# Attention denominators divided in the tail by rows spread through DRAM, and sigmoid gates computed in the prologue

## The chip, the cores and the metric

The kernel runs on one core of one Trainium2 chip. The metric is the device time of one execution in microseconds. The core has a matrix engine (TensorE; PE in the profile, PEld its weight loads), three engines for elementwise work (VectorE = DVE, ScalarE = ACT, GpSimd = POOL) and a queue engine that here only issues transfers (SyncE = SP; SPq for its DMA queue). Each engine works through its own instructions in order and waits on semaphores.

## What is computed

For a prompt of S = 2048 rows and D = 512 columns, with H = 32 heads of 16, a sliding window of 256, and a feed-forward part of F = 1792:

```python
q, k, v = split_heads(x @ wqkv)
scores = einsum("bhqd,bhkd->bhqk", q, k) * (Dh ** -0.5)
p = softmax(where((0 <= i - j) & (i - j < 256), scores, -1e9))
a = merge_heads(p @ v) @ wo                        # attention
b = (silu(x @ w_gate) * (x @ w_up)) @ w_down       # feed-forward
g = sigmoid((x * gate_w).sum(-1, keepdims=True))   # one gate per row
out = g * a + (1 - g) * b
```

## The kernel before

Everything is in float32, with operands split into a high and a low part, so that a product takes three matmuls (`mm3`, `products`). There are 16 blocks of 128 rows (NB), 4 column chunks of 512 (NCH, CH) and 8 groups of 4 heads (G). The order of each engine is the order in which the Python code issues its instructions; nothing reorders them later.

**Prologue (about 0 to 85 us).** x is loaded transposed, chunk by chunk, into the buffers that later hold the second pair of query and key stacks (slots `q10`, `q11`, `k10`, `k11`), and `split_x(c)` makes high and low parts of chunk c on ScalarE and VectorE. `proj` computes queries and keys for the first two head groups. `stack(g, hf)` writes their rows into the stacked layout by twelve transfers on SyncE. Then `stage1(0, ·)` starts: per block and head one scores matmul into a PSUM bank, then one VectorE instruction (line 304, `CUSTOM_DVE`) that masks it in place and takes the row maximum. For group 0 the four heads of a block alternate between two pools of two banks, so four score results can stand at a time; the matmul of the next block needs the bank of the block before. The value projections of the later blocks are interleaved.

**Main loop (to about 600 us).** It runs over t = 0 .. 128, 16 steps to a group. In a step `stage1` of the next group and `stage2` of this one (scores again with the maximum folded in, exponential on ScalarE, window cut on GpSimd) alternate with pieces of the feed-forward matmuls (line 252). Every fourth step `av` multiplies the probabilities with the values. The value tile has a column of ones, so row DH = 16 of each head's 32 rows is the softmax denominator. `finish(g, c)` takes the result of one chunk out of PSUM (lines 380 and 382), transposes it (386), divides by the denominator (390, 391), transposes it back (394) and writes it to DRAM, `od` (395, on GpSimd's queue). The function `later(t, hd, f)` puts work at a step t and a head position hd. In the last groups it places 16 gate blocks (line 631: a row block of x times gate_w, summed) and then `gate_end`, which makes the sigmoid and its complement and writes both to DRAM, `gd`.

**Tail (from about 600 us).** TensorE begins with the four `last_tile` products of the feed-forward part, 24 matmuls each. Meanwhile SyncE loads `wo`, the attention results (`load(e)`, from `od`) and the gate row spread over all partitions (`gates(0)`, 1 MB). `halve(e)` splits a loaded attention piece into high and low (ScalarE cast `hh`, VectorE subtraction `hl`), four items ahead of its use. The 16 items of `multiply_a` follow, twelve matmuls each, which TensorE starts at 622.77; `attn` multiplies their results by the gate (line 905) on VectorE and sends them to the output. Then come the items of the down projection, whose results `scaled` multiplies by 1 - gate (line 945) and adds into the output by the transfer.

```python
def load(e):
    _, c, k = e
    heads = od[2 * k:2 * k + 2].rearrange("g (j e) s -> (g j) e s", e=32)
    SRC[e] = taken(heads[:, :DH, c * CH:(c + 1) * CH])
```

An item's source is thus eight heads of sixteen rows, 512 columns each.

Of the kernel before, what the change touches and what calls it, by code (L numbers as in the profile page):

```python
# [16 lines left out]
P = 128  # L17
# [3 lines left out]
CH = 512  # L21
# [15 lines left out]
def gated_mix(ctx, tc, xT, xn, wqk, wv, wo, wgu, wd, gw, outT):  # L37
# [117 lines left out]
    gd = dram.tile([32, 4, 32], F32, name="gd")  # L155

# [44 lines left out]
    with ExitStack() as A:  # L201
# [170 lines left out]
        def finish(g, c):  # L372
# [5 lines left out]
            both, ot = AB[::-1] if c % 2 else AB  # L378
# [4 lines left out]
            if lo:  # L383
                nc.vector.tensor_copy(both[:, :lo], first[:, :lo])
            yield
            nc.vector.transpose(ot, both)
            yield
            v = ot.rearrange("p (s e) -> p s e", e=32)
            rc = osb.tile([P, CH // 32], F32, name="rc")
            nc.vector.reciprocal(rc, v[:, :, DH])  # L390
            nc.vector.tensor_tensor(out=v[:, :, :DH], in0=v[:, :, :DH],
                                    in1=rc[:, :, None].to_broadcast([P, CH // 32, DH]), op=ALU.mult)
            yield
            nc.vector.transpose(both, ot)
# [95 lines left out]
        split_x(2)  # L490
        for b in range(2, 4):
            run(vproj(b))
        run(proj(0, 1, pp, "pa"))
        stack(0, 0)
        split_x(3)
        QT.append([slot(f"q1{pr}") for pr in range(2)])
        KT.append([slot(f"k1{pr}") for pr in range(2)])
        for hf in range(2):
            fill_rows(QT[1], 0.0, hf, nc.gpsimd)
            fill_rows(KT[1], 1.0, hf, nc.gpsimd)  # L500
        run(proj(1, 1, pp, "pa"))
        for c in range(2, NCH):
            run(proj(0, c, pp, "pa"))
        stack(0, 1)
        stack(1, 0)

# [113 lines left out]
        XG = []  # L620

        def gate_place():
            xh, xl = x_pair()
            XG.extend(h.bitcast(F32) for t in (xh, xl) for h in halves_of(t))
            nc.sync.dma_start(XG[0], gw[None, :].to_broadcast([P, D]))

        def gate_fetch(b):
            nc.sync.dma_start(XG[2 + b % 2], xn[b * P:(b + 1) * P])

        def gate_block(b):  # L630
            nc.vector.scalar_tensor_tensor(XG[1], XG[2 + b % 2], 1.0, XG[0], op0=ALU.mult, op1=ALU.mult,
                                           accum_out=gate[:, b:b + 1])

# [24 lines left out]
        def gate_end():  # L658
            nc.scalar.activation(gate, gate, AF.Exp, scale=-1.0)
            nc.vector.tensor_scalar(gate, gate, 1.0, None, op0=ALU.add)  # L660
            nc.vector.reciprocal(gate, gate)
            nc.vector.tensor_scalar(igate, gate, -1.0, 1.0, op0=ALU.mult, op1=ALU.add)
            rows, cols = (sm.tile([P, 32], F32, name=n, bufs=1) for n in ("mt", "mtt"))
            nc.vector.tensor_copy(rows[:, :NB], gate)
            nc.vector.tensor_copy(rows[:, NB:], igate)
            nc.vector.transpose(cols, rows)
            nc.sync.dma_start(gd.rearrange("c q i -> q c i"), cols)

        blocks = [(t, n) for t in range(g7 - 8, g7 + NB, 4) for n in (range(1, 3) if t < g7 else range(3))][:NB]
        blocks = [(t + n, 3 - (n > 0)) for t, n in blocks]  # L670
        later(g7 - 11, 1, gate_place)
        for b in range(NB):
            t, hd = blocks[b]
            later(t, hd, lambda b=b: gate_block(b))
            if b > 1:
                t, hd = blocks[b - 2]
                later(t + hd // 3, (hd + 1) % 4, lambda b=b: gate_fetch(b))
            else:
                later(g7 - 10 + b, 2, lambda b=b: gate_fetch(b))
        later(g7 + NB - 2, 3, gate_end)  # L680
        for k in range(4):
            early(k)

        later(g7 + NB - 1, 3, lambda: later(g7 + NB, 0, prepare))
# [416 lines left out]
```

## Time and profile before

| what | value |
|---|---|
| median of 3 runs | 806.98 us (806.5 to 807.97) |
| the profiled execution | 805.57 us, its span 803.9 us |
| TensorE busy | 798.0 us (99%) |
| VectorE busy | 626.9 us (78%) |
| ScalarE busy | 432.4 us (54%) |
| GpSimd busy | 346.0 us (43%) |
| granted TensorE clock | 1.00 |
| DMA | 121.88 MB, mean 152 GB/s |

Rows of instruction groups read: line, engine, operation, output<-input, shape, count | busy us, mean ns of one | idle time of the engine ahead of them. Rows of the timeline read: start, duration, engine, line, operation, count [idle time ahead <- what ended it]. Rows of waits read: engine and its output <- engine that it waited for: total us, times, longest.

### The profile page before, as it was taken

The numbers are of one execution on the slowest core, as the hardware profiler recorded it, in microseconds if no ns is written. First come the engines' busy times: TensorE is split into PE (matmuls) and PEld (weight loads), VectorE is DVE, ScalarE is ACT, GpSimd is POOL, SyncE is SP. The second block draws the span as 40 slices with busy tenths as digits, with TensorE's granted clock in tenths as the row PEclk, the third lists the DMA queues.
The fourth block names the chain that finished last, engine by engine and source line by source line (L and its number), as shares of the span: only waits on it lengthen the run. The fifth ranks groups of instructions, "written<-read, shape, count | busy, mean of one in ns | idle before, by whom it ended". The sixth has DMA issues, their size and how long they took to land.

```text
span 803.9 us, 21546 instructions
## 1 busy us (share of the span) xinstructions
PE 798.0 (99%) x8251; PEld 679.7 (85%) x8251; DVE 626.9 (78%) x1685; ACT 432.4 (54%) x882; POOL 346.0 (43%) x647
## 2 busy tenths in 40 slices
PE   9999999999999999999999999999999999999997
PEld 7888998889888888888888988888878888888886
DVE  6397787868887787878777878888675478899896
ACT  7422556665566567555666556545643235554642
POOL 8812546555545456544656454546740111000212
PEclk9999999999999999999999999999999999999999
DMA  8584514435252453351444516435627898728535
GB/s 301 167 226 137 140 68 133 121 102 147 68 155 77 117 167 97 116 156 52 133 118 131 151 43 202 131 102 172 203 93 236 265 345 304 293 71 271 95 54 104
DMA packets 61963, 121.88 MB, mean 152 GB/s; under 512 B 10852, under 2 KB 19556, under 8 KB 61604
## 3 DMA queue, kind: packets, MB, share of 16 engines
q1 hardware_dynamic: 54756, 99.27, 40.2%
q0 software_dynamic: 7104, 21.24, 9.1%
q8 instruction: 65, 1.06, 0.6%
q14 instruction: 38, 0.31, 0.1%
HBM read 55.97 MB, written 39.34 MB: 119 GB/s over the span
## 4 chain that ended last, share of the span: by engine, by line
PE 98%; DVE 2%; issue 0%; POOL 0%; POOLq 0%
PE pa L252 24%; PE pb L252 24%; PE pb L365 7%; PE ps L302 6%; PE ps L341 5%; PE ps L88 4%; PE ps L89 4%; PE ps L90 4%; PE pa L232 2%; PE pb L232 2%; PE ps L365 2%; PE pb L88 2%; PE pa L88 2%; PE pa L89 2%; PE pb L89 2%; PE pb L90 2%
## 5 line engine op out<-in xcount | busy, mean ns | idle before, releaser
L304 DVE CUSTOM_DVE_ANT_0 ps<-ps,mask 128x384 f32<-128x384 f32 (+2 forms) x512 | 268.4, 540 | 102.4 <-PE ps L341 51.4
L343 ACT ACTIVATE pt<-ps 128x384 f32<-128x384 f32 (+2 forms) x512 | 238.0, 474 | 130.1 <-PE ps L302 66.3
L345 POOL TENSOR_SCALAR_AFFINE_SELECT pt<-pt 128x256 f32<-128x256 f32 x256 | 109.4, 428 | 200.2 <-ACT pt L343 199.7
L341 PE MATMUL ps<-q,k 64*128 64x384 f32 (+2 forms) x512 | 161.3, 333 | 0.0
L302 PE MATMUL ps<-k,q 63*128 63x384 f32 (+2 forms) x512 | 159.3, 331 | 0.5 <-DVE mx L304 0.5
L252 PE MATMUL pb<-xhi,wh 64*128 64x512 f32 x512 | 114.7, 395 | 0.0
L252 PE MATMUL pb<-xlo,wh 64*128 64x512 f32 x512 | 113.3, 391 | 0.0
L252 PE MATMUL pb<-xhi,wl 64*128 64x512 f32 x512 | 113.3, 391 | 0.0
L252 PE MATMUL pa<-xhi,wh 64*128 64x512 f32 x512 | 113.2, 394 | 0.0
L252 PE MATMUL pa<-xlo,wh 64*128 64x512 f32 x512 | 111.8, 391 | 0.0
L252 PE MATMUL pa<-xhi,wl 64*128 64x512 f32 x512 | 111.8, 391 | 0.0
L302 PEld LDWEIGHTS ps<-k,q 63*128 63x128 f32 x512 | 88.7, 184 | 17.1 <-issue 5.7
L348 POOL TENSOR_SCALAR_AFFINE_SELECT pt<-pt 128x256 f32<-128x256 f32 x224 | 98.4, 439 | 0.0
L341 PEld LDWEIGHTS ps<-q,k 64*128 64x128 f32 x512 | 90.5, 184 | 5.8 <-issue 0.8
L365 PE MATMUL ps<-pt,vg 64*32 64x320 f32 (+4 forms) x1408 | 75.0, 346 | 0.0
L365 PE MATMUL pb<-pt,vg 64*32 64x320 f32 (+3 forms) x1360 | 73.9, 350 | 0.0
L304 DVE DVE_READ_ACCUMULATOR2_ANT mx<- 128x1 f32 x512 | 71.4, 139 | 0.0
L365 PEld LDWEIGHTS pb<-pt,vg 64*32 64x32 f32 x1360 | 46.4, 106 | 28.1 <-DVE mx L304 5.1
L252 PEld LDWEIGHTS pb<-xhi,wh 64*128 64x128 f32 x512 | 60.4, 185 | 5.4 <-DVE o L382 0.2
L252 PEld LDWEIGHTS pb<-xhi,wl 64*128 64x128 f32 x512 | 60.1, 184 | 4.9
L252 PEld LDWEIGHTS pa<-xhi,wl 64*128 64x128 f32 x512 | 58.7, 184 | 5.5
L252 PEld LDWEIGHTS pa<-xhi,wh 64*128 64x128 f32 x512 | 58.7, 186 | 3.7
(305 smaller groups left out, 1629.8 us busy)
## 6 DMA issues: line engine op xcount, KB each, us to landing
kept_h<-ev SPq DMA_DIRECT2D x52, 256.0 KB
od<-o POOLq DMA_DIRECT2D x32, 256.0 KB, 3.8
raw<-wgu SPq DMA_DIRECT2D x28, 256.0 KB
q<-xhi SPq DMA_DIRECT2D x56, 128.0 KB
k<-xhi SPq DMA_DIRECT2D x56, 128.0 KB
outT<-sg POOLq DMA_DIRECT2D x28, 256.0 KB, 4.0
vd<-vs POOLq DMA_DIRECT2D x8, 672.0 KB, 4.8
vg<-vd SPq DMA_DIRECT2D x32, 168.0 KB
```

The lines of the kernel that those rows point to most:

```text
L88: nc.tensor.matmul(ps, lh, rh, start=start and i == 0, stop=False, skip_group_check=skip)
L89: nc.tensor.matmul(ps, lh, rl, start=False, stop=False, skip_group_check=skip)
L90: nc.tensor.matmul(ps, ll, rh, start=False, stop=stop and i == n - 1, skip_group_check=skip)
L232: nc.tensor.matmul(ps, w, x, start=n == 0, stop=n == len(todo) - 1)
L252: mm = nc.tensor.matmul(ps[me], w[r], x[r], start=not second and i == 0, stop=bool(second) and i == n - 1)
L302: nc.tensor.matmul(ps[:, :n], QT[g % 2][pr][r, q0:q0 + P], KT[g % 2][pr][r, k0:k0 + n], start=True, stop=True)
L304: mx = nc.vector.tensor_tensor_reduce(out=ps[:, :n], in0=ps[:, :n], in1=mask[:, 3 * P - n:], scale=1.0, scalar=NEG, op0=ALU.add, op1=ALU.m ...
L341: nc.tensor.matmul(ps[:, :n], KT[g % 2][pr][r, k0:k0 + P], QT[g % 2][pr][r, k0:k0 + n], start=True, stop=True)
L343: BEHIND.append(nc.scalar.activation(pt[:, j, :n], ps[:, :n], AF.Exp, scale=SCALE))
L345: nc.gpsimd.affine_select(out=pt[:, :, :P], in_=pt[:, :, :P], pattern=[[0, 2], [1, P]], compare_op=ALU.is_ge, fill=0.0, base=0, channel_mu ...
L348: nc.gpsimd.affine_select(out=pt[:, :, 2 * P:], in_=pt[:, :, 2 * P:], pattern=[[0, 2], [-1, P]], compare_op=ALU.is_ge, fill=0.0, base=-1, ...
L365: nc.tensor.matmul(AV[g, c][h][32 * j:32 * j + 32, q0 - c * CH:q1 - c * CH], VG[4 * g + kb // 4][o, kb % 4, 17 * j:17 * j + 32], PT[g, kb, ...
```

## The change

`finish` no longer transposes and divides: it writes the undivided sums with the denominators to `od`. For each group three new steps run one after another: `get_den` reads the denominators of four heads from `od` into a tile of 128 x 64, `invert_den` takes the reciprocal and multiplies it by the gate (`grow`, laid out alike), `put_den` writes the result to DRAM, `rd`, one row per head. For groups 0 to 6 this happens in the main loop after the group; for group 7 in the tail. In the tail, `inverse(e)` loads eight rows of `rd`, each spread over 16 partitions, and `halve(e)` multiplies the attention piece by it before splitting. `attn` becomes a ScalarE copy, and `gates(0)` with its 1 MB load goes.

Since the gate is now needed early, it is computed in the prologue. The slot `q10` serves as gate_w and three fetch buffers (`gx`), so its fill with zeros moves behind `gate_end`. Nine gate blocks stand behind `split_x(2)`, seven behind `split_x(3)`.

```diff
+    rd = dram.tile([H, S], F32, name="rd")
+    def get_den(g):
+        nc.sync.dma_start(den, od[g].rearrange("(j e) (u s) -> j e u s", e=32, s=64)[:, DH])
+    def invert_den():
+        nc.vector.reciprocal(den, den)
+        nc.vector.tensor_tensor(out=den, in0=den, in1=grow, op=ALU.mult)
+    def put_den(g):
+        nc.sync.dma_start(rd[4 * g:4 * g + 4].rearrange("j (u s) -> j u s", s=64), den)
...
-            nc.vector.transpose(ot, both)
-            v = ot.rearrange("p (s e) -> p s e", e=32)
-            rc = osb.tile([P, CH // 32], F32, name="rc")
-            nc.vector.reciprocal(rc, v[:, :, DH])
-            nc.vector.tensor_tensor(out=v[:, :, :DH], in0=v[:, :, :DH],
-                                    in1=rc[:, :, None].to_broadcast([P, CH // 32, DH]), op=ALU.mult)
-            nc.vector.transpose(both, ot)
             nc.gpsimd.dma_start(od[g, :, c * CH:(c + 1) * CH], both)
...
         split_x(2)
+        gx = [h for t in halves_of(slot("q10", F32)) for h in halves_of(t)]
+        nc.sync.dma_start(gx[0], gw[None, :].to_broadcast([P, D]))
+        def gate_blocks(bs, ahead):
+            for b in bs:
+                t = gx[1 + b % 3]
+                nc.vector.scalar_tensor_tensor(t, t, 1.0, gx[0], op0=ALU.mult, op1=ALU.mult, accum_out=gate[:, b:b + 1])
+                if b + 3 < ahead:
+                    gate_fetch(b + 3)
+        for b in range(3):
+            gate_fetch(b)
+        gate_blocks(range(9), 9)
         for b in range(2, 4):
             run(vproj(b))
         run(proj(0, 1, pp, "pa"))
         stack(0, 0)
+        for b in range(9, 12):
+            gate_fetch(b)
         split_x(3)
+        gate_blocks(range(9, NB), NB)
...
+        gate_end()
         stack(0, 1)
         stack(1, 0)
+        nc.sync.dma_start(grow, gd[:NB].rearrange(...))
...
+        for g in range(G - 1):
+            t = (g + 1) * NB
+            later(t + 4, 2, lambda g=g: get_den(g))
+            later(t + 6, 2, invert_den)
+            later(t + 7, 2, lambda g=g: put_den(g))
...
+        def inverse(e):
+            _, c, k = e
+            z_place(4 * (c % 2), 0)
+            SRC[e] = SRC[e], PLACE["z", 2 * (c % 2)][:, k]
+            nc.sync.dma_start(SRC[e][1],
+                              rd[8 * k:8 * k + 8, c * CH:(c + 1) * CH][:, None].to_broadcast([8, DH, CH]))
...
         for e in ITEMS[:LEAD]:
             load(e)
-        gates(0)
+        for e in ITEMS[:LEAD - 1]:
+            inverse(e)
         store = last_tile(0)
...
+        get_den(G - 1)
         last_tile(1)
+        invert_den()
         store()
+        put_den(G - 1)
         for f in late[2:]:
             f()
+        for e in ITEMS[LEAD - 1:AHEAD]:
+            inverse(e)
...
+            if n + 8 < WO:
+                inverse(ITEMS[n + 8])
```

How the order of the engines moves: in the rows below, the numbers of buffers stand behind the names; `k_...` on the right are the raw x chunks, `ps_...` the PSUM banks of the scores. VectorE in the prologue, from the third x split to the first score maximum, before:

```order
L73 TENSOR_TENSOR xlo_76<-k_145,xhi_75 128x512 x4
L73 TENSOR_TENSOR xlo_78<-k_146,xhi_77 128x512 x4
L304 ISA ps_474,mx<-ps_474,mask 128x128
L304 ISA mx 128x1
L304 ISA ps_477,mx<-ps_477,mask 128x128
```

The same stretch of VectorE now (line 316 is the former 304):

```order
L73 TENSOR_TENSOR xlo_76<-k_148,xhi_75 128x512 x4
L504 SCALAR_TENSOR_TENSOR q_297,gate<-q_297 128x512 x9
L73 TENSOR_TENSOR xlo_78<-k_149,xhi_77 128x512 x4
L504 SCALAR_TENSOR_TENSOR q_297,gate<-q_297 128x512 x7
L510 TENSOR_SCALAR gate<-gate 128x16
L511 RECIPROCAL gate<-gate 128x16
L512 TENSOR_SCALAR igate<-gate 128x16
L514 COPY mt<-gate 128x16
L515 COPY mt<-igate 128x16
L516 STREAM_TRANSPOSE mtt<-mt 128x32
L316 ISA ps_522,mx<-ps_522,mask 128x128
```

The sixteen gate blocks and the six operations of `gate_end` now stand ahead of the first score maximum.

SyncE in the tail, from its first load on, before:

```order
L738 DMA got<-wo 128x512 x4
L738 DMA got<-od 128x1x512 x4
L890 DMA k_10639<-gd 128x2048
L738 DMA got<-od 128x1x512 x2
L776 DMA kept_h<-q_10667 128x512
L738 DMA got<-od 128x1x512 x4
L776 DMA kept_h<-q_10667 128x512
L738 DMA got<-od 128x1x512 x2
L185 DMA xlo_10821<-wd 128x512 x2
```

SyncE in the tail now (`rd` the spread inverse rows, `den` the denominators of the last group):

```order
L744 DMA got<-wo 128x512 x4
L744 DMA got<-od 128x1x512 x4
L839 DMA q_10510<-rd 128x1x512 x3
L744 DMA got<-od 128x1x512 x2
L160 DMA den<-od 128x1x64
L782 DMA kept_h<-q_10540 128x512
L167 DMA rd<-den 128x64
L839 DMA q_10510<-rd 128x1x512
L839 DMA k_10592<-rd 128x1x512 x2
L744 DMA got<-od 128x1x512 x4
L782 DMA kept_h<-q_10540 128x512
L839 DMA k_10592<-rd 128x1x512 x2
```

The load of `den` is the fourteenth transfer of the tail, and the spread loads stand between the loads of `od`.

VectorE in the tail, from the second `last_tile` on, now:

```order
L780 SCALAR_TENSOR_TENSOR k_10579<-k_10579,pa 128x512
L781 SCALAR_TENSOR_TENSOR k_10579<-k_10579,pb 128x512
L163 RECIPROCAL den<-den 128x64
L164 TENSOR_TENSOR den<-den,grow 128x64
L73 TENSOR_TENSOR wol<-got,woh 128x512 x2
L780 SCALAR_TENSOR_TENSOR q_10540<-q_10540,pa 128x512
L781 SCALAR_TENSOR_TENSOR q_10540<-q_10540,pb 128x512
L846 TENSOR_TENSOR got<-got,q_10510 128x512
L73 TENSOR_TENSOR hl<-got,hh 128x512
L846 TENSOR_TENSOR got<-got,q_10510 128x512
```

Before, the lines 163, 164 and 846 were not there; the two `wol` splits followed the second `last_tile` at once.

More of the change, by code (lines that the diff above doesn't have):

```diff
@@ L155, in gated_mix @@
     gd = dram.tile([32, 4, 32], F32, name="gd")
+    rd = dram.tile([H, S], F32, name="rd")
+    grow, den = (const.tile([P, 64], F32, name=n) for n in ("grow", "den"))
+    def get_den(g):
[5 more added lines that the diff above has]
+        nc.sync.dma_start(rd[4 * g:4 * g + 4].rearrange("j (u s) -> j u s", s=64), den)
     def half_sign(f, c):
@@ L503, in gated_mix @@
             run(proj(0, c, pp, "pa"))
+        gate_end()
+        for hf in range(2):
+            fill_rows(QT[1][:1], 0.0, hf, nc.gpsimd)
         stack(0, 1)
         stack(1, 0)
+        nc.sync.dma_start(grow, gd[:NB].rearrange("c q i -> (c q i)").rearrange("(u s) -> u s", s=64)[None].to_broadcast([4, 32, 64]))
         first = chain(*(stage1(0, b) for b in range(NB)))
@@ L619, in gated_mix @@
         g7 = (G - 1) * NB
[L620 to L632, printed above, removed]
         def early(k):
@@ L656, in early @@
             later(t - 1, 2, lambda: later(t, 3, rest))
[L658 to L680, printed above, removed]
+        for g in range(G - 1):
[3 more added lines that the diff above has]
+            later(t + 7, 2, lambda g=g: put_den(g))
         for k in range(4):
@@ L999, in gated_mix @@
             halve(e)
+        for e in ITEMS[AHEAD:8]:
+            inverse(e)
         rows = [(p, k) for p in ORDER if p in STAGES for k in range(4, NP)]
```

44 lines of the change are left out of this document (29 added, 15 removed).

## The prediction

> **What bounds the kernel now.** I read the busy times and the granted clock first, then the chain that ended last, then the waits.
>
> ```profile
> PE 798.0 (99%) x8251; PEld 679.7 (85%) x8251; DVE 626.9 (78%) x1685; ACT 432.4 (54%) x882; POOL 346.0 (43%) x647
> PEclk9999999999999999999999999999999999999999
> PE 98%; DVE 2%; issue 0%; POOL 0%; POOLq 0%
> PE ps L302 <- DVE mx L304: 0.5, 2, 0.2
> ```
>
> TensorE is busy for 798.0 of 803.9 us at full clock, and the chain lies on it for 98%. The change touches none of its instructions, so it can only shorten or lengthen TensorE's waits. The last row (time, count, longest) says how little there is to shorten: in all the main loop TensorE stood visibly still for VectorE twice, 0.5 us together. VectorE, at 78%, is not the bound. A place where TensorE must wait for a new chain is therefore a loss at almost full price, and there are two candidates: the prologue and the start of the tail.
>
> **Part 1, taken out of `finish` (main loop).** These are the groups that go, busy time and mean ns:
>
> ```profile
> L386 DVE STREAM_TRANSPOSE o<-o 128x512 f32<-128x512 f32 x32 | 22.6, 705 | 0.0
> L394 DVE STREAM_TRANSPOSE o<-o 128x512 f32<-128x512 f32 x32 | 22.5, 703 | 0.2
> L391 DVE TENSOR_TENSOR o<-o,rc 128x256 f32<-128x256 f32 x32 | 17.0, 531 | 1.1
> L390 DVE RECIPROCAL rc<-o 128x16 f32<-128x16 f32 x32 | 7.9, 248 | 0.0
> ```
>
> That is 22.6 + 22.5 + 17.0 + 7.9 = 70.0 us of VectorE, 2.19 us for each of 32 pieces. What TensorE gets of it is only the stalls that these instructions cause. The timeline has the largest kind:
>
> ```profile
> 201.11 1.15 DVE L391 TENSOR_TENSOR o<-o,rc 128x256 f32<-128x256 f32 x1
> 202.23 0.39 PE L252 MATMUL pa<-xhi,wl 64*128 64x512 f32 x2
> 202.85 0.44 PE L302 MATMUL ps<-k,q 63*128 63x384 f32 x1 [0.23 <-DVE mx L304]
> ```
>
> One multiplication took 1.15 instead of 0.53 us, the maximum behind it came late, and the next scores matmul began at 202.85 instead of 202.23 + 0.23 (its neighbours follow at 0.23): 0.39 us lost. Twice that is 0.8. A start-to-start gap that is a little long isn't listed as a wait; I allow 0.4 for those. Bounds: 0 (other VectorE work takes the blame) to 3. I take **-1.2**. Seven small reciprocals, seven multiplications (each at most the 0.25 of L390) and their 14 small transfers come back, in a loop that has just lost 2.19 us of VectorE at 28 places: nothing. The transposed-out piece reaches `od` 2 us sooner, which nobody waits for until the tail. The 16 gate blocks leave the last groups, where TensorE did not wait for them: nothing.
>
> **Part 2, gates in the prologue.** VectorE now does, between the third and fourth x split, nine gate blocks, then behind the fourth split seven more, then `gate_end`'s exponential on ScalarE and six operations of VectorE, and only then the first maximum (L304 of before). SyncE issues fetches 9 to 11 only behind the twelve `stack` transfers.
>
> ```profile
> 9.91 4.80 SPq L465 DMA_DIRECT2D k<-xT  x8
> 15.14 0.33 SPq L78 DMA_DIRECT2D raw<-wgu  x1
> 34.29 0.59 SPq L286 DMA_DIRECT2D k<-xhi  x1
> 1.25 0.42 SPq L465 DMA_DIRECT2D q<-xT  x1
> 3.96 0.62 ACT L70 CAST xhi<-q 128x512 fp32r<-128x512 f32 x1 [0.86 <-DMA q<-xT]
> L631 DVE SCALAR_TENSOR_TENSOR xhi<-xlo,xhi 128x512 f32<-128x512 f32 x16 | 11.0, 690 | 1.7 <-DMA xlo<-xn 1.7
> L631 DVE DVE_READ_ACCUMULATOR xhi<-xlo,xhi 128x1 f32 x16 | 1.3, 79 | 0.0
> 594.33 0.07 DVE L631 DVE_READ_ACCUMULATOR xhi<-xlo,xhi 128x1 f32 x1
> 596.01 0.21 DVE L666 STREAM_TRANSPOSE mtt<-mt 128x32 f32<-128x32 f32 x1
> 37.07 0.30 DVE L304 CUSTOM_DVE_ANT_0 ps<-ps,mask 128x128 f32<-128x128 f32 x1 [6.11 <-POOL x10lo L73]
> 38.80 0.28 PE L302 MATMUL ps<-k,q 63*128 63x256 f32 x2
> od<-o POOLq DMA_DIRECT2D x32, 256.0 KB, 3.8
> ```
>
> The last `stack` transfer is issued at 34.29 and takes 0.59, so fetch 9 goes out at about 35.5 (a little SyncE time of the sixteen added issues included). A 256 KB load of this shape took 3.96 - 1.25 = 2.7 us from issue to use. One block costs 0.69 + 0.08 = 0.77. Three buffers turn the seven blocks into a chain of three loads: 35.5 + 2.7 = 38.2, block 9 until 39.0, fetch 12 lands 41.7, block 12 until 42.5, fetch 15 lands 45.2, block 15 until 46.0. The gate's end took from 594.40 (end of the last block) to 596.22, 1.8, so 47.8; the first maximum needs 0.30 more: 48.1. Before, that maximum began at 37.07. Four score results fit in PSUM, so TensorE's first four matmuls go through, and the fifth, which began at 38.80, needs a result bank that only the first maximum frees. 48.1 - 38.8 = **+9.3**, less 0.1 for the interleaved value projections that can run ahead: **+9.2**. Lower bound, all loads perfectly side by side: 38.2 + 7 x 0.77 + 1.8 + 0.3 = 45.7, +6.9. Upper, every load at the 3.8 us of the last row: 35.5 + 3 x (3.8 + 0.77) + 2.1 = 51.3, +12.5. I stay near the row with the same shape and queue.
>
> The first nine blocks cost nothing of their own:
>
> ```profile
> 18.98 2.50 DVE L73 TENSOR_TENSOR xlo<-k,xhi 128x512 fp32r<-128x512 f32 x4
> 31.47 0.39 PE L232 MATMUL pa<-xlo,wh 128*128 128x512 f32 x1
> ```
>
> VectorE is free from 21.48, and TensorE first needs the fourth split at 31.47. The eighth fetch lands in the third wave, 15.5 + 1 + 3 x (2.7 + 1.5) = 29 to 30, so the split is up to 1 us late; the larger stall behind it absorbs that. The later fills and stacks move too, but their readers come some 20 us later.
>
> **Part 3, the last group's denominators at the start of the tail.** SyncE's queue in the timeline (start, issue time, count):
>
> ```profile
> 601.01 2.77 SPq L738 DMA_DIRECT2D got<-wo  x4
> 603.89 2.90 SPq L738 DMA_DIRECT2D got<-od  x4
> 607.15 0.51 SPq L890 DMA_DIRECT2D k<-gd  x1
> 607.78 1.28 SPq L738 DMA_DIRECT2D got<-od  x2
> 609.16 0.82 SPq L776 DMA_DIRECT2D kept_h<-q  x1
> 610.60 6.99 SPq L738 DMA_DIRECT2D got<-od  x4
> 612.94 0.57 SPq L738 DMA_DIRECT2D got<-od  x1
> 619.29 0.32 SPq L776 DMA_DIRECT2D kept_h<-q  x1
> 620.43 1.82 SPq L738 DMA_DIRECT2D got<-od  x2
> 622.73 1.08 SPq L185 DMA_DIRECT2D xlo<-wd  x2
> 625.07 0.59 SPq L738 DMA_DIRECT2D got<-od  x1
> 622.77 0.39 PE L88 MATMUL ps<-hh,woh 128*128 128x512 f32 x1
> ```
>
> SyncE rotates eight semaphores; a transfer goes out when the one eight places ahead has landed. The 14th of the tail went out at 612.94 (when the 6th had landed), the 22nd at 625.07, so the 14th landed at about 625.0. In those 12.1 us the 7th to 14th landed: six `od` loads, the 1 MB of `gd` and one store. At the prologue's pace of (15.14 - 9.91) / 8 = 0.65 per 256 KB, `gd` and the store are 2.6 + 0.65, which leaves (12.1 - 3.25) / 6 = **1.48 us for an `od` load**, more than twice the pace. Its shape is eight heads of sixteen rows. The new `rd` load is eight rows spread sixteen times, and the trace of before has none. Bounds: 0.65 as an ordinary 256 KB load (`gd`, also a spread one, ran at that), 1.48 as `od`. I take 1.48, because its outer side is the same eight.
>
> [...]
>
> Now the 14th transfer is the new `den` load, behind four `wo`, four `od`, three `rd` and two more `od`. From 612.94: seven loads of 1.48 and about 1 for its 64-element rows, 624.3. (At 0.65 for `rd`: 621.8.) VectorE waits there in order, and behind the division stand two `wo` splits, two operations of the third last tile, the first multiplication, then a cast on ScalarE:
>
> ```profile
> 615.44 0.69 DVE L774 SCALAR_TENSOR_TENSOR q<-q,pa 128x512 f32<-128x512 f32 x1 [1.46 <-ACT q L773]
> 615.30 1.65 ACT L70 CAST hh<-got 128x512 fp32r<-128x512 f32 x3
> ```
>
> With 0.5 for the division and its product, 2 x 0.65 + 2 x 0.69 + 0.69 + 0.6 = 4.0: 4.5 us in all, so TensorE's first attention item starts at 628.8 instead of 622.77: **+6.0**. Bounds: 2, if the `rd` loads are cheap and half the queue behind the division is done ahead of it, to 8, if `den` with its short rows lands 2 us later.
>
> **Part 4, the rest of the tail.** 1 MB of `gd` goes, 16 `rd` loads come; 16 products leave VectorE for ScalarE copies and 16 multiplications come to VectorE, so VectorE's sum is unchanged, and ScalarE (54%) has room: nothing. The transfers are another matter:
>
> ```profile
> 640.00:660.00 20.00, 20.00 (x90) 16.57 (x89) 14.58 (x25) 6.96 (x12) 3.78 (x7) 1.00 0.96 340
> ```
>
> The last two columns are the DMA engines' busy share and GB/s: 0.96 already. From 628.5 until item 15's row must be there, 13 `rd` and 10 `od` loads at 1.48 and about 22 ordinary ones (stores, `wd`, x parts, results) at 0.65 have to land: 34.0 + 14.3 = 48.3, to 676.8. An item is twelve matmuls at 0.227 (the 0.23 above), 2.72; item 15 would start 15 x 2.72 after 628.8, at 669.6, and needs its row 2.6 earlier (multiplication, cast, subtraction, place in line): 667. Some of the ordinary transfers can go later, so of the 9.8 I take **+7**. Bounds 0 (cheap `rd`) to 10.
>
> **The sum.** 805.57 (profiled execution: span 803.9 and 1.67 around it) - 1.2 + 9.2 + 6.0 + 7 = 826.6. The median of the runs, 806.98, is 1.4 above the profiled one: **828.0**.
>
> **The rivals.** A, the sum as it stands, 823 to 833: chance 0.50. B, the start of the tail is late but the later loads keep up, because the ordinary transfers are not ahead of the `rd` loads: 821, 817 to 823, chance 0.20; for it speaks that nobody waits soon for the stores and x parts, against it the 0.96 above. Rival three, `rd` at 0.65: start of the tail +3.4, later 0, 805.57 - 1.2 + 9.2 + 3.4 + 1.4 = 818.4, inside B's span. C, the tail hides everything, since `den` lands before the last tiles are done: 805.57 - 1.2 + 9.2 + 1.4 = 815, 811 to 817, chance 0.15; against it stands the queue's eight-place rule. D, short rows and doubled loads make the tail worse than A: 833 to 845, chance 0.09. E, on the other side: VectorE's gate chain in the prologue is done before the fifth score matmul is due, with fetches landing as fast as they are issued and VectorE through by 38.8; then only -1.2 is left and perhaps a tail whose wait the four last tiles cover: 805.57 - 1.2 + 1.4 = 805.8. It decides if fetch 15 lands before about 36, and the twelve `stack` issues alone end at 34.9; chance 0.06.
>
> **How the numbers follow.** About 0.2% (1.6 us) is what this measurement can tell from no change. The point is A's, 828. The range 813 to 833 leaves out D, E and a few hundredths of C. Faster 0.03 and same 0.03 are E's halves, slower is A to D, 0.94.
>
> **What would show it.** TensorE's waits should show one of about 9 us near 39 whose releaser is VectorE's maximum or gate operations, and one of about 6 us at 623, behind the `den` load; the first maximum should stand at 47 to 48. Waits of SyncE-loaded rows in the multiplications should grow through the items up to 670. The prediction is wrong if the second set of gate blocks is done before 39, if `den` lands before 618, or if `rd` loads pass at 0.65.

## The result: 840.6 us, slower by 4.2%

The changed kernel takes 840.57 us (839.88 to 843.38, four runs) against 807.16 before; ratio 1.042, 95% interval 1.0393 to 1.0447. The forecast was 828.0 with a range to 833. The profiled execution took 839.88 us, 34.3 us more than the 805.57 of the profile before.

The page after, in its busy times, granted clock and chain:

```profile
PE 808.1 (96%) x8251; PEld 691.5 (83%) x8251; DVE 591.2 (71%) x1573; ACT 440.7 (53%) x898; POOL 336.2 (40%) x647
PEclk9979999999999999999999999999999989999999
PE 86%; DMA 9%; DVE 2%; SPq 1%; ACT 1%; issue 0%; ACTq 0%
```

VectorE has lost 36 us of work, and TensorE is busy 10 us longer with the same 8251 matmuls: in two places its clock is below full. The chain of before lay on TensorE for 98%; now DMA has 9% of it. The waits (the fourth row is one of VectorE's) name the places:

```profile
PE ps L314 <- DVE mx L316: 8.5, 1, 8.5
PE pa L244 <- DVE xlo L73: 3.0, 1, 3.0
PE ps L88 <- ACT hh L70: 2.3, 1, 2.3
DVE den L163 <- DMA den<-od: 7.7, 1, 7.7
PE ps L88 <- ACT sg L923: 5.5, 2, 2.9
PE pb L88 <- ACT sg L923: 3.7, 2, 2.3
```

TensorE's instructions stand in the same order in both kernels, so the start of one and the same matmul can be subtracted. That tells where the 34.3 us arose (an ordinary table, worked out from the starts of TensorE's instructions):

| matmul's start before | late by, just ahead | late by, at it | late when the matmuls have their pace again |
|---|---|---|---|
| 31.47 (fourth x split) | 0.9 | 4.0 | 5.5 |
| 38.80 (fifth scores matmul) | 5.5 | 14.2 | 17.1 |
| 62 to 622 (main loop) | 17.1 | 15.9 | 15.9 |
| 622.77 (first attention item) | 15.9 | 18.4 | 20.6 |
| 646 (item 8, third and fourth bank) | 20.6 | 26.8 | 28.5 |
| 657 (item 12, third and fourth bank) | 28.5 | 32.6 | 34.3 |

So 17.1 us belong to the prologue, -1.2 to the loop and 18.4 to the tail. (The expectations below reckon with -0.9 and 18.1.) Of the 17.1, 0.9 stand there before the first new instruction; in the runs below whose prologue is that of before it is 0.2 to 0.8, so the change's own share is about 16.2. The last column shows something that was not in the forecast: behind each stall TensorE loses 1.5 to 2.9 us more. A table by stretches shows why (columns: stretch, its length, busy time and count of each engine, granted clock, DMA share, GB/s):

```profile
35.50:39.00 3.50, 3.49 (x9) 2.81 (x10) 1.76 (x3) 0.00 (x0) 1.68 (x2) 0.58 0.74 206
53.00:61.00 8.00, 8.00 (x49) 8.00 (x51) 4.70 (x23) 0.36 (x1) 0.00 (x0) 0.63 0.61 148
61.00:70.00 9.00, 9.00 (x86) 9.00 (x84) 8.63 (x31) 2.31 (x5) 3.09 (x3) 1.00 0.90 260
641.00:646.00 5.00, 4.66 (x12) 3.49 (x13) 3.53 (x6) 1.80 (x4) 0.00 (x0) 0.66 0.45 134
673.30:678.00 4.70, 4.67 (x14) 3.74 (x15) 2.18 (x5) 1.11 (x2) 1.08 (x2) 0.64 0.85 289
690.00:696.00 6.00, 5.99 (x19) 4.77 (x20) 3.48 (x6) 4.67 (x10) 1.63 (x3) 0.72 1.06 393
```

Behind a stall the clock is 0.58 to 0.72 for some microseconds. Five such stretches, each its length times the clock that is missing, sum to 1.5 + 3.0 + 1.7 + 1.7 + 1.7 = 9.5 us.

The prologue in the timeline, SyncE, VectorE, TensorE:

```profile
17.00 14.16 SPq L499 DMA_DIRECT2D q<-xn  x9
31.25 0.58 SPq L297 DMA_DIRECT2D q<-xhi  x1
38.95 8.16 SPq L499 DMA_DIRECT2D q<-xn  x7
34.77 2.49 DVE L73 TENSOR_TENSOR xlo<-k,xhi 128x512 fp32r<-128x512 f32 x4
35.51 0.80 PE L244 MATMUL pa<-xlo,wh 128*128 128x512 f32 x1 [2.97 <-DVE xlo L73]
42.04 0.73 DVE L504 SCALAR_TENSOR_TENSOR q<-q 128x512 f32<-128x512 f32 x1 [4.78 <-DMA q<-xn]
52.59 0.29 DVE L316 CUSTOM_DVE_ANT_0 ps<-ps,mask 128x128 f32<-128x128 f32 x1
52.99 0.83 PE L314 MATMUL ps<-k,q 63*128 63x256 f32 x2 [8.53 <-DVE mx L316]
```

The nine fetches with three buffers keep SyncE until 31.16, so the `stack` transfers, which stand behind them, start at 31.25 instead of 27.27, and fetch 9 goes out at 38.95, not at 35.5. VectorE reaches the fourth split only at 34.77. The first maximum is at 52.59; the forecast had it through at 48.1.

The tail:

```profile
627.23 0.52 SPq L160 DMA_DIRECT2D den<-od  x1
628.46 1.68 SPq L782 DMA_DIRECT2D kept_h<-q  x1
637.20 0.33 SPq L167 DMA_DIRECT2D rd<-den  x1
636.36 0.55 DVE L163 RECIPROCAL den<-den 128x64 f32<-128x64 f32 x1 [7.66 <-DMA den<-od]
641.12 0.50 PE L88 MATMUL ps<-hh,woh 128*128 128x512 f32 x1 [2.27 <-ACT hh L70]
667.30 0.69 DVE L846 TENSOR_TENSOR got<-got,q 128x512 f32<-128x512 f32 x1 [2.50 <-DMA q<-rd]
668.10 0.62 ACT L70 CAST hh<-got 128x512 fp32r<-128x512 f32 x1 [3.54 <-DVE got L846]
668.62 0.58 ACT L923 COPY sg<-ps 128x512 f32<-128x512 f32 x1
669.25 0.50 PE L88 MATMUL ps<-hh,woh 128*128 128x512 f32 x1 [2.61 <-ACT sg L923]
```

From the issue of the denominators' load to TensorE's first item is the chain that the forecast had; the landing at 636.3 is 620.4 in the time of before (15.9 less). SyncE issues nothing from 630.1 to 637.2. The last four rows show a late stall: TensorE needs a PSUM bank, the copy that frees it stands behind a cast, the cast behind a multiplication, and that behind a row of `rd`.

### The profile page after: what moved, and what is told of

Read it like the earlier page. It is cut to its first block, busy times and chain, and to the rows that moved or that the text cites. A ratio compares the mean times of both kernels' runs of the same rounds, so it can differ in the third digit from the quotient of the medians.

```text
span 838.2 us, 21494 instructions
## 1 busy us (share of the span) xinstructions
PE 808.1 (96%) x8251; PEld 691.5 (83%) x8251; DVE 591.2 (71%) x1573; ACT 440.7 (53%) x898; POOL 336.2 (40%) x647
## 4 chain that ended last, share of the span: by engine, by line
PE 86%; DMA 9%; DVE 2%; SPq 1%; ACT 1%; issue 0%; ACTq 0%
PE pb L264 23%; PE pa L264 23%; PE pb L377 7%; PE ps L314 6%; PE ps L353 5%; DMA got<-od 3%; PE ps L89 3%; PE ps L88 3%; PE ps L90 3%; PE pb L244 2%; PE ps L377 2%; DMA q<-rd 1%; PE pb L88 1%; PE pb L89 1%; PE pb L90 1%; PE pa L89 1%
## 5 line engine op out<-in xcount | busy, mean ns | idle before, releaser
L316 DVE CUSTOM_DVE_ANT_0 ps<-ps,mask 128x384 f32<-128x384 f32 (+2 forms) x512 | 272.3, 544 | 130.7 <-PE ps L314 73.0
L357 POOL TENSOR_SCALAR_AFFINE_SELECT pt<-pt 128x256 f32<-128x256 f32 x256 | 105.5, 413 | 215.3 <-ACT pt L355 212.8
L314 PE MATMUL ps<-k,q 63*128 63x384 f32 (+2 forms) x512 | 162.9, 332 | 8.5 <-DVE mx L316 8.5
L314 PEld LDWEIGHTS ps<-k,q 63*128 63x128 f32 x512 | 92.8, 186 | 22.2 <-DVE mx L316 9.4
L360 POOL TENSOR_SCALAR_AFFINE_SELECT pt<-pt 128x256 f32<-128x256 f32 x224 | 93.9, 419 | 0.0
```

Source lines behind the costliest of these rows:

```text
L314: nc.tensor.matmul(ps[:, :n], QT[g % 2][pr][r, q0:q0 + P], KT[g % 2][pr][r, k0:k0 + n], start=True, stop=True)
L316: mx = nc.vector.tensor_tensor_reduce(out=ps[:, :n], in0=ps[:, :n], in1=mask[:, 3 * P - n:], scale=1.0, scalar=NEG, op0=ALU.add, op1=ALU.m ...
L357: nc.gpsimd.affine_select(out=pt[:, :, :P], in_=pt[:, :, :P], pattern=[[0, 2], [1, P]], compare_op=ALU.is_ge, fill=0.0, base=0, channel_mu ...
L360: nc.gpsimd.affine_select(out=pt[:, :, 2 * P:], in_=pt[:, :, 2 * P:], pattern=[[0, 2], [-1, P]], compare_op=ALU.is_ge, fill=0.0, base=-1, ...
```

## Experiments

Differences are to the runs of before on the same chip (806.5 to 807.3 us). Gains of single edits are taken against the changed kernel's 840.6, which was measured at another time (before took 807.16 then), and the runs of one such kernel spread by 1 to 5 us; so a gain under about 2 us is not clear of noise.

**Each half alone.** First the gates alone in the kernel before, then the division alone:

```diff
 # e1, on the kernel before
         split_x(2)
+        ... gx, gate_fetch, gate_blocks(range(9), 9), as in the change
         split_x(3)
+        gate_blocks(range(9, NB), NB)
...
+        gate_end()
 # e2, on the changed kernel: gate blocks and gate_end back in the last groups
-        nc.vector.tensor_tensor(out=den, in0=den, in1=grow, op=ALU.mult)
```

> The kernel before with only the gates moved into the prologue (same code and places as in the changed kernel); division, tail and gate multiplication stay as before. My theory: the loss of the change is two separate losses, and the prologue's is 17.1 us by the two traces (TensorE's matmuls are 17.1 us late at the end of the prologue), so about 807 + 17 = 824 us (823 to 826), with TensorE standing still near 32 and near 44 us and running at about 0.6 of its clock for some us behind each. Rival: the tail of before has slack in its transfers that swallows part of the prologue's delay, or the prologue's delay needs the rest of the change: then under 818.

> The changed kernel with the gates back in the last groups as before; the inverse denominators are made and spread as in the change, but the gate is left out of them (the attention part of the output isn't multiplied by the gate). My theory: the prologue's 17.1 us are gone, the tail's 18.1 and the loop's -0.9 remain: 807 + 17 = 824 us (822 to 827). Rival: the tail's loss comes from the late start of the gate chain or from changed timing only, then under 815.

Measured: 822.75 us, ratio 1.0205 (1.019 to 1.022), and 824.18, ratio 1.0215 (1.0198 to 1.0232). That is +16.3 and +17.7, together 34.0, against 33.4 for the whole change. Both are as expected (e1 by 0.25 under its range). The two losses are separate and add up; neither hides behind the other.

**Does a stall cost more than its length?** Idle VectorE instructions ahead of the first score maximum, in the kernel before (the zero fill of `q10` moves behind them):

```diff
         split_x(3)
+        gx = [h for t in halves_of(slot("q10", F32)) for h in halves_of(t)]
+        nc.vector.memset(gx[0], 0.0)
+        nc.vector.memset(gx[2], 0.0)
+        for _ in range(14):        # 22 in e4
+            nc.vector.tensor_tensor(out=gx[1], in0=gx[0], in1=gx[2], op=ALU.mult)
```

> The kernel before with nothing of the change, but 2 fills and 14 idle multiplications (128 x 512) on VectorE between the fourth x split and the first score maximum. VectorE is free there from 31.0; 0.9 + 14 x 0.605 + 0.5 brings the first maximum to its end at about 40.9, so TensorE stands still for about 2.1 us at its fifth scores matmul. My theory that a stall also costs TensorE half its clock for some us afterwards: about +4 us in all (3.5 to 5), if 2 us are enough to trip it. Rival, a stall costs its own length: +2.1, clock 1.00 throughout.

> The same with 22 multiplications: the first maximum ends at about 45.7, TensorE stands still for about 6.9 us. My theory (the stall and half the clock afterwards for 3.4 to 7 us): +9 to +10 us, granted clock near 0.6 behind the stall. Rival, a stall costs its own length: +6.9.

Measured: 816.03 (+9.6) and 821.83 (+15.4). Both stalls were longer than planned, since the multiplications were slower (the last section). The waits, and the stretches behind the stalls, first with 14, then with 22:

```profile
PE ps L302 <- DVE mx L304: 7.0, 3, 6.5
...
PE ps L302 <- DVE mx L304: 12.8, 3, 12.3
```

```profile
46.20:54.00 7.80, 7.78 (x57) 7.78 (x59) 5.59 (x25) 1.08 (x2) 1.60 (x2) 0.78 0.58 143
...
51.70:58.00 6.30, 6.27 (x32) 6.27 (x34) 3.53 (x18) 0.00 (x0) 1.60 (x2) 0.51 0.54 133
58.00:66.00 8.00, 8.00 (x76) 8.00 (x75) 7.22 (x27) 2.67 (x5) 2.74 (x3) 1.00 0.65 197
```

Stalls of 6.5 and 12.3 us cost 9.6 and 15.4: about 3 us over their length. The sizes that I had expected were missed; the rival (a stall costs its length, with the clock at 1.00) is refuted by the clock. But the time lost at the low clock differs: 7.8 x 0.22 = 1.7 us behind the shorter stall, 6.3 x 0.49 = 3.1 behind the longer one. The rest of the shorter one's 3 us is not at the stall: by the subtraction of starts TensorE loses another 1.2 us in the main loop, where nothing was edited, and why stays open. Whether 2 us suffice is not shown by these two. Two runs below show that at about 2 us it goes either way: the wait ahead of the first attention item and the clock behind it, in e2 and in e7:

```profile
PE ps L88 <- ACT hh L70: 2.2, 1, 2.2
626.50:636.00 9.50, 9.27 (x40) 7.41 (x41) 6.64 (x11) 2.99 (x5) 0.00 (x0) 1.00 0.52 165
...
PE ps L88 <- ACT hh L70: 1.9, 1, 1.9
641.30:646.30 5.00, 4.76 (x13) 3.54 (x14) 3.63 (x6) 1.74 (x3) 0.00 (x0) 0.66 0.84 159
```

A wait of 2.2 us left the clock at 1.00, one of 1.9 us was followed by 0.66.

**The prologue's steps.** Nine fetch buffers instead of three, so that no fetch waits for a block (e8; the fills of these slots move behind the gate's end), and then the last seven blocks and the gate's end between the score maxima (e11):

```diff
-        gx = [h for t in halves_of(slot("q10", F32)) for h in halves_of(t)]
+        gx = [h for n in ("q10", "q11", "k10") for t in halves_of(slot(n, F32)) for h in halves_of(t)]
-            nc.sync.dma_start(gx[1 + b % 3], xn[b * P:(b + 1) * P])
+            nc.sync.dma_start(gx[1 + b % 9], xn[b * P:(b + 1) * P])
 # e11 besides: in the loop over the first group's score maxima
+            if n < 7:
+                gate_blocks(range(9 + n, 10 + n), NB)
+            if n == 6:
+                gate_end()
...
```

> The changed kernel with one edit: nine fetch buffers for the gate blocks (slots q10, q11 and k10) instead of three, so that SyncE issues the fetches without waiting and the stack transfers start at about 27.5 instead of 31.2. My theory: the stall at 32 us goes, the last seven blocks come without the chain of three loads and end near 44, the first maximum near 46; the prologue then costs 7.4 + 2 to 3 instead of 17: 840.6 - 7 = 833.5 us (831 to 836). Rival, VectorE's own work and the loads' landing set the end of the gate chain, whatever the buffers: 838 to 841.

> The changed kernel with nine fetch buffers in the prologue, and the last seven gate blocks and the gate's end put between the score maxima of the first group, so that no maximum stands behind them all. The tail is as in the changed kernel. My theory: the prologue's 17.1 us become 0 to 2: 807.3 + 1 - 0.9 + 18.1 = 825.5 us (823 to 829). Rival: VectorE has no room between the maxima, and TensorE waits there as long as before: 832 or more.

Measured: 835.78 us (ratio 1.0353, 1.0326 to 1.038) and 830.79 (1.0304, 1.0285 to 1.0324). With nine buffers SyncE and TensorE read:

```profile
27.85 0.57 SPq L297 DMA_DIRECT2D q<-xhi  x1
...
35.55 3.40 SPq L501 DMA_DIRECT2D q<-xn  x7
```

```profile
47.49 0.83 PE L314 MATMUL ps<-k,q 63*128 63x256 f32 x2 [7.47 <-DVE mx L316]
```

The stall at 32 us is gone and fetch 9 goes out at 35.55, where the forecast had put it (35.5). So it was the held queue that had moved it. The fifth scores matmul starts at 47.49, near the forecast's 48.1, but by another way: with nine buffers the chain of three loads is gone too. The prologue's loss falls from 17.1 to 10.7, by the same subtraction of starts. The time fell by 4.8 only, at the edge of what was expected, as this profile's tail lost 19.8 us. In e11 the expected gain was missed: the prologue still loses 7.4 us, 5.0 of them at one place (a wait of 2.5 us and the half clock behind it), where VectorE does the last block and the gate's end while score results wait. VectorE works there without a gap, as the rival said, but the wait is shorter than the rival's.

**The tail's steps, one edit each.** GpSimd's queue for the last group's denominators; a pending result copy ahead of the next cast; each row of `rd` written twice, so that a spread load has sixteen outer rows; all four copies of a chunk at once:

```diff
-        get_den(G - 1)                                  # e5
+        get_den(G - 1, nc.gpsimd)
-        put_den(G - 1)
+        put_den(G - 1, nc.gpsimd)
...
+            first = n < WO and JOBS                     # e6
+            if first:
+                JOBS.pop(0)()
             if n + LEAD < len(ITEMS):
                 halve(ITEMS[n + LEAD])
...
-    rd = dram.tile([H, S], F32, name="rd")              # e7
+    rd = dram.tile([H, 2, S], F32, name="rd")
-                     ...[:, None].to_broadcast([8, DH, CH])
+                     ...[:, None].to_broadcast([16, DH // 2, CH])
...
+            while JOBS and n < WO + 1:                  # e9
+                JOBS.pop(0)()
             if n + LEAD < len(ITEMS):
                 halve(ITEMS[n + LEAD])
```

> The changed kernel with one edit: the last group's denominators are read from and written to DRAM through GpSimd's queue instead of SyncE's, so SyncE isn't held by the write that waits for VectorE (in the changed kernel it issued nothing from 630.1 to 637.2). My theory: the denominators land near 627 instead of 636.3, no stall at 638, and the loads behind start 6 to 7 us earlier; 4.3 us of stall and half clock go, and some of the 14 us later: 840.6 - 7 = 833.5 us (831 to 836). Rival, the loads in the tail are limited by the DMA engines alone and the held queue costs nothing more: only the first stall goes, 836.5; if the start doesn't matter since the later wait grows by as much, 840.

> The changed kernel with one edit in the order: in the attention items of the tail the pending result copy (which frees a PSUM bank) is issued ahead of the next item's multiplication and cast, not behind them. In the trace TensorE's three late stalls (669, 673, 687) end with a copy on ScalarE that stood behind a cast, and the cast behind a multiplication that waited for a row of rd. My theory: the rows are needed four items later than the copies make it seem, so 840.6 - 7 = 833.5 (831 to 836). Rival, the rows are late for TensorE too: 839 to 841.

> The changed kernel with one edit: each inverse row is written to DRAM twice, so that a spread load of rd has sixteen outer rows instead of eight. Eight outer rows took 1.27 us each in the tail's landing times, and their semaphore counted nine steps instead of sixteen. Theory: the load's outer side sets how many DMA engines work on it; with sixteen it lands at the 0.65 of an ordinary 256 KB load, 16 x 0.62 = 10 us of transfer time go, the denominators land about 2 us earlier, and most of the late stalls shrink: 832 us (829 to 836). Rival, the loads' price isn't in their shape but in the held SyncE queue: 838 to 841, and landing times of 1.27 as before.

> The changed kernel with one edit: when an attention column chunk is done, its four copies out of PSUM are issued at once, ahead of the next item's multiplication and cast (in the run with one copy a step ahead, a copy still stood behind the casts of the steps between). In the trace of the changed kernel an item's low part is ready at 661 (item 8) and 677 (item 12), while TensorE starts them at 665 and 691, so the rows are there and the banks are not. My theory: the three late stalls behind the banks go, and what is left is item 15's row, ready at 690.2 where TensorE would be at 684: 14 us of late loss become about 6: 840.6 - 7 = 833 us (830 to 836). Rival: the rows are what is late and the copies only stand in the way of the same wait: 838 to 841.

Measured: 838.30, 839.07, 835.95 and 838.43 us, gains of 2.3, 1.5, 4.6 and 2.1 where about 7 to 9 had been expected of each. In e5 the stall at 638 goes, and half of its 4.7 us come back later. SyncE is held all the same, now by the next spread load, which needs the row that is being written:

```profile
SPq L839 <- DMA rd<-den: 8.3, 1, 8.3
```

So e5 does not test what a free queue would bring. e6 and e9 end where their rivals put them. In e9 the bank stalls go (no wait for the copies is left) and casts that wait for rows take their place, at items 12 to 14. My theory that the copies' place makes the stalls falls: the rows are late, and the copy stands in the way of the same wait. In e7 the first spread loads landed 0.75 to 0.9 apart instead of 1.3, by the events of their semaphores, and it gained most, just within its range.

**Both sets together.** e10 has all tail edits and the `od` loads that wait for nothing ahead of the `rd` loads that do; e12 adds e11's prologue.

> The changed kernel with all four tail edits: the denominators of the last group by GpSimd's queue, rows of rd in sixteen, the four copies at once, and the od loads that depend on nothing ahead of the rd loads that do. The prologue is as in the changed kernel. My theory: the tail's 18.1 us become 3 to 6: 807.3 + 17.1 - 0.9 + 4.5 = 828 us (825 to 831). Rival: the tail is limited by the sum of its transfers, whatever their order: 833 or more.

> Both sets of edits, prologue and tail. My theory, the two parts add up: 807.3 + 1 - 0.9 + 4.5 = 812 us (808 to 816); the division by rows of rd is then about as fast as before and not faster, since VectorE's relief of 70 us is worth 0.9. Rival: a part is hidden under the other and the sum is worse than its parts: above 818.

Measured: 828.27 us (1.0265, 1.0248 to 1.0282) and 820.15 (1.0158, 1.0132 to 1.0184). e10 is as expected: the tail's loss falls from 18.4 to 7.7 us. e12 is above its expectation by 8, since the prologue still costs 9.8 in its trace, and its runs spread from 816.4 to 821.3. It is not that one part hides under the other: e11's prologue, e10's tail and the loop are 7.4 + 7.7 - 1.2 = 13.9, and e12 lost 13.5. No version that divides in the tail beats the kernel before.

**What is it about the tail?** The division alone (e2), and from it: no division at all (e13, the ceiling), the rows loaded but not used (e14), the spread loads without the last group's chain (e15), the chain without the loads (e16):

```diff
-                nc.vector.tensor_tensor(out=src, in0=src, in1=r, op=ALU.mult)   # e13, e14, e16
-            inverse(e)                                                          # e13, e16, at all four places
-        get_den(G - 1)                                                          # e13, e15
-        invert_den()
-        put_den(G - 1)
+                later(t + 7, 3, lambda: put_den(G - 1))                         # e15, once, in the loop
```

> The run with the division only, and from it the division itself taken out (no denominators are read, inverted, written or spread; the attention part is neither divided nor multiplied by the gate; the result copies stay on ScalarE). It is the ceiling: VectorE has 70 us less, and nothing is paid for it. My theory: 806.6 - 1 = 805.6 us (804.5 to 806.5), because TensorE waits for VectorE only a few tenths at a time in the loop. Rival: VectorE's load slows the loop in more ways than its waits show, 803 or less.

> The run with the division only, and from it one line out: the attention pieces aren't multiplied by the rows of rd, which are still read, inverted, written, spread and loaded in the same order (the attention part is neither divided nor gated). Nothing then waits for a row of rd but SyncE's queue and the division waiting for the last group's denominators. Theory A, the tail's 17.7 us come from the chain through the rows (landing, multiplication, cast, copy): about 806.6 + 4 = 811 us (809 to 813), with the start of the items late by the denominators' wait, and the late stalls at items 8 and 12 gone. Theory B, from the load on the transfer engines and SyncE's held queue, by which the od loads come late as well: 817 or more.

> The run with the division only, without the last group's chain in the tail: its rows of rd are written ahead of time in the loop, with group 6's denominators in their place (so heads 28 to 31 are divided by wrong denominators, and the gate is left out). All sixteen spread loads and the multiplications stay. It tells the volume of the spread loads from the held queue. Theory V (volume: sixteen loads of 1.27 us more on the engines that already carry the od loads): 806.5 + 10 = 816 us or more. Theory H (SyncE held from the last store to the inverse's write, 7 to 9 us): 806.5 + 4 = 811 us or less.

> The counterpart: the run with the division only, with the last group's chain (read, invert, write) in its place, but without the spread loads and the multiplications (the attention part is neither divided nor gated). Theory V: the chain alone costs what its wait costs TensorE, 0 to 3 us: 806 to 809. Theory H: SyncE held for some 7 us makes the od loads late, 811 or more. If the two runs' losses add up to less than the 17.7 of both together, it is the one behind the other that costs.

| run | what the tail has | us | against before | ratio, 95% |
|---|---|---|---|---|
| e13 | neither loads nor chain | 805.71 | -0.8 | 0.9989 (0.9979 to 0.9998) |
| e16 | the chain alone | 805.78 | -0.8 | 0.9991 (0.9982 to 1.0) |
| e15 | the spread loads alone, used | 818.24 | +11.7 | 1.0152 (1.0135 to 1.0169) |
| e2 | both, used | 824.18 | +17.7 | 1.0215 (1.0198 to 1.0232) |
| e14 | both, rows not used | 822.74 | +16.3 | 1.0197 (1.0181 to 1.0212) |

The chain alone costs nothing, though VectorE waits in it:

```profile
DVE den L163 <- DMA den<-od: 3.6, 1, 3.6
```

The sixteen loads with their use cost 11.7 + 0.8 = 12.5 us. The chain on top of them costs 6.0 more. By the traces its load then stands behind three of them: `den` lands at 622.0 in e2 and at 616.4 in e16, and SyncE is held until the row is written, with 13 spread loads and 10 `od` loads behind it. No edit takes this hold away by itself, so that it is the whole of the 6.0 is not shown. Using the rows is worth 1.4 at most (the intervals of e14 and e2 overlap). In e14 TensorE's one long stall has another name:

```profile
669.81 0.62 ACT L70 CAST xlo<-got 128x512 fp32r<-128x512 f32 x1 [11.01 <-DMA got<-wd]
...
671.48 0.79 PE L88 MATMUL pb<-hh,woh 128*128 128x512 f32 x1 [12.19 <-ACT sg L923]
```

Here a load of `wd`, which the change doesn't touch, is what comes late: the whole queue is. Theory B was right and theory A wrong, and of e15 and e16 it was theory V both times (e16 0.2 under its range).

## Why the prediction was right or wrong

**Right: the bound and the relief.** 70 us less of VectorE bring 0.8 us (e13; 0.2 to 1.7 by its interval) and 1.2 in the loop of the changed kernel, where -1.2 was forecast with bounds of 0 and -3. **Right: the two places and their sign.** The prologue and the tail cost, separately.

The other terms, forecast and measured: prologue +9.2 and 17.1, start of the tail +6.0 and 4.7, rest of the tail +7 and 13.7. The misses sum to 13.3, which is 839.88 - 826.6.

**Wrong: the prologue's term, +9.2, measured 17.1.** The step that failed is "fetch 9 goes out at about 35.5". It counted the blocked SyncE nowhere: the ninth fetch waits for VectorE's sixth block, and the `stack` transfers stand behind it. Fetch 9 went out at 38.95, 3.5 us later. The chain behind it took 1.4 us longer than worked out: the last block ended 11.3 us after the issue of fetch 9, not 10.5, and the gate's end took 2.4, not 1.8. Then come 2.9 us of half clock: 9.3 + 3.5 + 1.4 + 2.9 = 17.1. The fourth split was late by 3.1 us and not "up to 1", but that the larger stall absorbs this was right: the fifth scores matmul starts when the first maximum is through, and nothing in VectorE's chain to it waits for TensorE. That e8 comes within 0.6 us of the forecast's 48.1 is partly luck: its seven blocks end at 44.0, not 46.0, and its gate's end took 3.1 us, not 1.8.

**Wrong in size: the start of the tail, +6.0, measured 2.4 and 2.2 behind it, most of that half clock.** The chain behind the landing was right (4.5 forecast, 641.12 - 636.36 = 4.8 measured). The landing came 4 us earlier than worked out. The seven loads landed 1.24 to 1.33 apart here and not 1.48 (in the trace of before the six `od` loads of the derivation landed 1.1 to 2.3 apart, 1.5 in the mean), `den` itself added 0.25 and not 1, and its load went out 1.7 us sooner. The choice to price `rd` as `od` was right: 1.24 to 1.33 for the first three `rd` loads, 1.24 to 1.29 for the `od` loads about them. (The third rival's +3.4 is 3.5 by its own figures, 621.8 + 4.5 - 622.8.) The semaphores of the `od` and `rd` loads, which have eight outer rows, counted nine steps here, that of `den` five, and those of the prologue's `xT` loads, which land 0.64 apart in the mean, sixteen. With sixteen outer rows (e7) the count was sixteen. How many DMA engines work on such a load, which e7's theory spoke of, no trace of this case shows.

**Wrong: the rest of the tail, +7, measured 13.7, and its path.** The sum of transfers had given 9.8 and I took 7 of it; the runs show 10.3 of stalls and 3.4 of half clock. e15 confirms the kind of the term, transfers and not arithmetic. The step that failed is taking part of it off because "some of the ordinary transfers can go later": eight transfers are in flight in order (before, the fourteenth of the tail went out at 612.94, just after the sixth had landed at 612.86), so a later one that must wait also holds those behind it. The write of `rd` was such a one, and my working had named it only as a wait of VectorE. The chain added 6.0 us (e2 against e15), by the two traces 3.0 of it at the start of the items and 3.1 behind. That the untrimmed 9.8 is near the 10.3 is partly luck. The transfers took as long as worked out (from 638.7 to the landing of item 15's row at 687.0, 48.4 us against 48.3), but they began at 622.7 in the time of before, not at 628.5, and it is not this row that TensorE waited for:

```profile
689.50 0.69 DVE L73 TENSOR_TENSOR hl<-got,hh 128x512 fp32r<-128x512 f32 x1 [0.74 <-ACT hh L70]
697.89 0.39 PE L88 MATMUL pa<-hh,woh 128*128 128x512 f32 x1
```

Item 15 is ready at 690.2 and TensorE takes it at 697.9. It had stopped before, at the banks of items 8 and 12, whose copies stand behind casts that wait for the rows of later items.

**Missing: what a stall does to the clock.** Every stall was priced at its length. By the granted clock 9.5 us were lost behind the five stalls, but not all of it was extra time: the 1.5 at 36 us lie ahead of a stall that ends when VectorE is through, whatever TensorE did before. The 3.0 behind the prologue's large stall and the 1.7 behind the last one have no stall after them that could absorb them, so 4.7 us at least, and 8.0 at most, of the 12.6 by which the forecast was too low are half clock. The trace shows the half rate in the matmuls too: 0.427 us from one to the next at 36 us against 0.227, with a granted clock of 0.50 from 35.5 to 38.4. What sets it off is not shown: waits of 1.9 us (e7), 2.27 (641.12) and 2.97 us (35.51) were followed by it and one of 2.2 us (e2) was not. Nor is it one length: by the clock of the stretches above, half speed lasted from 2 x 3.5 x 0.42 = 2.9 us to 2 x 6.3 x 0.49 = 6.2 us behind a stall. (e4's expectation reckoned with 3.4 to 7 us; in the changed kernel's trace the granted clock is 0.50 from 642.6 to 645.9 and from 669.9 to 676.7.)

## What to carry to other kernels

Where the matrix engine is at 99%, work taken from another engine is worth only the waits it ended (here 70 us for 0.8), while each new wait that no later one absorbs costs its length and often 1.5 to 3 us of half clock more (here behind waits of 1.9 us and longer, though not behind one of 2.2). When transfers are added to an in-order queue, price the whole queue: which transfers stand behind one that waits, how many are in flight, and how long each load of that shape takes by its landings. A load whose outer side is eight rows costs about twice an ordinary one of the same size (1.24 to 1.33 us against 0.65 here), and a fetch that waits for its buffer holds everything that is issued after it (here the `stack` transfers, from 27.27 to 31.25).

## What the runs showed of the hardware

The clock is treated above. The other surprise is in the run with 14 idle multiplications, VectorE and GpSimd (start, duration or sum, count):

```profile
35.03 4.10 DVE L500 TENSOR_TENSOR q<-q 128x512 f32<-128x512 f32 x3
41.58 2.15 DVE L500 TENSOR_TENSOR q<-q 128x512 f32<-128x512 f32 x3
```

```profile
35.41 1.48 POOL L73 TENSOR_TENSOR x10lo<-ev,x10hi 128x512 fp32r<-128x512 f32 x1
36.84 1.74 POOL L73 TENSOR_TENSOR x01lo<-ev,x01hi 128x512 fp32r<-128x512 f32 x1
```

The same three VectorE multiplications take 4.10 us beside GpSimd's subtractions and 2.15 when GpSimd is idle. GpSimd's fills with a constant, just before, did not slow them (2.15 for the three from 32.85 on). Why the two slow each other is not shown. The multiplication of 1.15 us that the forecast quoted from the main loop (201.11) may be the same: in the trace of before GpSimd's subtraction lies beside it. No edit tested it.

```profile
200.69 1.29 POOL L73 TENSOR_TENSOR xlo<-ev,xhi 128x512 fp32r<-128x512 f32 x1
```
